# Attention, MoE and soft MoE on one core: the second pair's norm, the third pair's squares, two weight blocks and the first output block moved

## The chip, the cores and the metric

The kernel runs on one core of a Trainium2 chip. The time is device microseconds from the launch's start to its end on that core; a run is compared with other runs of the same kernel by the median. The engines are PE (TensorE, matrix products), DVE (VectorE), ACT (ScalarE), POOL (GpSimd) and SP (SyncE, which here only issues transfers). Transfers are issued from SP, ACT and POOL.

## What the reference computes

```python
# q, k, v: (4, 12, 448, 64); w_in (768, 2048), w_out (2048, 768); phi (768, 32); w1 (8, 768, 1024), w2 (8, 1024, 768)
q_n, k_n = rmsnorm(q, g_q), rmsnorm(k, g_k)
attn = softmax(q_n @ k_n.T / sqrt(64))          # with the row maximum subtracted
x = (attn @ v) as (1792, 768)
x = relu(x @ w_in) ** 2 @ w_out
logits = x @ phi
d = softmax over the 1792 tokens of logits       # dispatch
slot_input = d.T @ x                             # 32 slots, 4 for each of 8 experts
slot_out[e] = relu(slot_input[e] @ w1[e]) @ w2[e]
out = softmax over the 32 slots of logits @ slot_out
```

Everything is float32.

## The kernel before

**Attention** runs over 24 pairs of heads (4 batches, 6 pairs in each). A pair goes through these steps; the names are those of `blocks` in `attention()`:

- `load` brings q and k of a pair into two tiles `qk` (4 buffers, so a load waits until the norm has used the tiles of two pairs before).
- `norm` computes 1/rms. `inverse_rms` squares on ACT (line 250, tile `sq`, one buffer), reduces on DVE (252, `ss`), scales (258, `ms`), makes a first guess `y` by integer arithmetic on ACT (259), and takes three Newton steps of three DVE operations each (261 to 263). Then it multiplies q and k by y (302, `qs`). The first two pairs are done singly, later ones two at a time (`together`).
- `trans0`, `trans1` transpose on PE and make the operands of a head: `m1`/`m2` hold the rounded value of q and its remainder, `s1`/`s2` those of k with the gains. For the first pair `trans_first` does it: `m1` and its copy, `s1` and its remainder, then `gate` (a write that holds back the conversion of weights), then the "low" parts, `m2` on DVE (291) and `s2` on ACT (292). For later pairs the copies `m<-m` and `s<-s` are transfers on SP (331, 339).
- `max0`, `max1` (`rowmax`) compute the scores' row maxima: products on PE, a reduce on DVE (389, `nm`).
- `row0`, `row1` (`maxrow`) transpose the maxima (395), cast them (397, `mt`) and send them by a transfer into row 64 of `m2` (398), on ACT's queue for the first pair and on SP's for all others.
- `s00` to `s11` are the scores with the exponentials (411, tile `p`, 2 buffers), `v00` to `v11` the products with v, `recip` and `out` the division by the row sums.

`ORDER` and the first number in `blocks` set in which sequence the steps of neighbouring pairs are emitted. The framework's scheduler then fixes the order on each engine at compile time: it takes what was emitted first among what its own model of the times holds to be ready. So an instruction that was emitted late can stand early in an engine's queue, and on the chip the queue waits for it. Copies of a single element (248, 257, 364, 365) only exist to put one instruction behind another in this order.

**Weights.** `w_in` and `w_out` are fetched in 32 blocks of 768 KB by transfers on POOL's queue (`fetch64`), as raw words; `convert` turns a block into a high and a low part on ACT and DVE (553, 554, 560, 561), and SP writes these to scratch in DRAM. The list `CONVERT` says at which steps of attention a block is converted. The first four blocks (`PD`) are fetched with the first load, behind a one-element copy on POOL that waits for the first k. While attention goes on, the first layer (`moe_hidden`) is filled in between its steps, paced by `PACE`.

**The last part.** When attention's buffers are given back, three pools of buffers (`ring`, 18; `ring3`, 3; `ring2`, 5) take pieces of the weights in a fixed order, each piece in the buffer of one that is done (`done`, `fetch`). When no piece is left to fetch, `done` appends the pool to the list `free`. `finish` makes the output in 12 blocks `ob`, each in a buffer of the pool that it takes from the head of `free`; a block is copied out of PSUM in two halves by ACT and DVE (1158, 1156), and SP sends it (1159). By the order of the pieces the list begins with one entry of `ring`, then five of `ring2`, then five of `ring`, then `ring3`.

Of the kernel before, what the change touches and what calls it, by code (L numbers as in the profile page):

```python
# [8 lines left out]
F32 = mybir.dt.float32  # L9
# [11 lines left out]
def raw(ap):  # L21
    return ap.bitcast(F32)
# [19 lines left out]
VF, PD, LEAD, SLOPE = 9, 4, 1.5, 0.75  # L42
WF, EARLY, NTOP = 4, 1, 1
LAG, GATE, MTQ = 1, 1, 1
DUPE, HIP, SELG, VC, AHEAD = 0, 0, 1, 0, 1
FIRST = "load norm trans0 trans1 max0 max1 row0 row1 s00 s01 s10 s11".split()


ON_PL = [1, 0, 1, 1, 1, 1, 1, 1, 1, 1, 1, 0, 1, 0, 0, 1]
# [12 lines left out]
def tile_attention_moe_softmoe(  # L62
# [144 lines left out]
    def load_v(t):  # L207
        b, hp = divmod(t, NP)
        vh, vl = vst[t % 2]
        if t < VF:  # L210
            vf = att.tile([CP, 2, NC, D + 1], F32, tag="vr", name=f"vf_{t}", bufs=2)
            nc.vector.memset(vf[:, :, :, D:], 1.0)
            live[t]["vf"] = vf
            if VC:

                vr = att.tile([CP, 2, S], F32, tag="pl", name=f"vr_{t}", bufs=2)[:, :, : NC * D]
                nc.sync.dma_start(vr, v[b, 2 * hp : 2 * hp + 2].rearrange("h (p c) d -> p h (c d)", c=NC))
                nc.gpsimd.tensor_copy(vf[:, :, :, :D], vr.rearrange("p h (c d) -> p h c d", c=NC))
                return
            for j in range(2):  # L220
                nc.sync.dma_start(
                    vf[:, j, :, :D], v[b, 2 * hp + j].rearrange("(p c) d -> p c d", c=NC)
                )
            return
        vr = att.tile([CP, 2, NC, D + 1], F32, tag="vr", name=f"vr_{t}", bufs=2)
        vr = vr.rearrange("p h c d -> p (h c d)")[:, : 2 * NC * D].rearrange("p (h c d) -> p h c d", h=2, c=NC)
        nc.sync.dma_start(
            vr.rearrange("p h c d -> p h (c d)"),
            v[b, 2 * hp : 2 * hp + 2].rearrange("h (p c) d -> p h (c d)", c=NC),
        )  # L230
        for j in range(2):
# [9 lines left out]
    def inverse_rms(ts):  # L241
        n = 16 * len(ts)
        ss = att.tile([CP, 32], F32, tag="ss", name=f"ss_{ts[0]}", bufs=1)[:, :n]
        for x, t in enumerate(ts):
            for i in range(2):
                sq = att.tile([CP, 8, D], F32, tag="sq", name=f"sq_{t}_{i}", bufs=1)
                if AHEAD and t == 1 and i == 0:
                    nc.vector.tensor_copy(sq[0:1, 0, 0:1], live[0]["qs"][1][0:1, 0, 0, 0:1])
                qf = live[t]["qk"][i].rearrange("p h c d -> p (h c) d")
                nc.scalar.activation(sq, qf, AF.Square)  # L250
                at = 16 * x + 8 * i
                nc.vector.tensor_reduce(ss[:, at : at + 8], sq, AX.X, ALU.add)  # L252
        ms = att.tile([CP, 32], F32, tag="ms", name=f"ms_{ts[0]}", bufs=1)[:, :n]
        y = att.tile([CP, 32], F32, tag="y", name=f"y_{ts[0]}", bufs=2)[:, :n]
        u = att.tile([CP, 32], F32, tag="u", name=f"u_{ts[0]}", bufs=1)[:, :n]
        if AHEAD and ts[0] == 1:
            nc.vector.tensor_copy(ms[64:65, 0:1], raw(operands(0, 1)["s1"][64:65, 0:1]))
        nc.vector.tensor_scalar(ms, ss, 1.0 / D, EPS, ALU.mult, ALU.add)
        nc.scalar.activation(y.bitcast(I32), ms.bitcast(I32), AF.Copy, bias=float(0x5F3759DF), scale=-0.5)
        for _ in range(3):  # L260
            nc.vector.scalar_tensor_tensor(u, y, -0.5, y, ALU.mult, ALU.mult)
            nc.vector.tensor_tensor(u, u, ms, ALU.mult)
            nc.vector.scalar_tensor_tensor(y, u, 1.5, y, ALU.add, ALU.mult)
        for x, t in enumerate(ts):
            live[t]["y"] = y[:, 16 * x : 16 * x + 16]


    def trans_first():
        pss = []
        for i in range(2):  # L270
            ps = mps()
            x = live[0]["qs"][i]
            for c in range(NC):
                nc.tensor.transpose(
                    ps[:, c * CP : (c + 1) * CP], x[:, c].rearrange("p h d -> p (h d)"), ident[:CP, :CP]
                )
            pss.append(ps)
        for j in range(2):
            o = operands(0, j)
            h = slice(64 * j, 64 * j + 64)  # L280
            m, s, g = pss[0][h, :S], pss[1][h, :S], gkq[h, :]
            nc.scalar.copy(o["m1"][0:64, :], m)
            nc.vector.tensor_copy(o["m1"][64:128, :], m)
            nc.scalar.activation(o["s1"][0:64, :], s, AF.Copy, scale=g)
            nc.vector.scalar_tensor_tensor(o["s1"][64:128, :], s, g, raw(o["s1"][0:64, :]), ALU.mult, ALU.subtract)
        if GATE:
            gate(raw(o["s1"][64:65, 0:1]))
        for j in range(2):
            o = operands(0, j)
            h = slice(64 * j, 64 * j + 64)  # L290
            nc.vector.tensor_tensor(o["m2"][0:64, :], pss[0][h, :S], raw(o["m1"][0:64, :]), ALU.subtract)
            nc.scalar.activation(o["s2"][0:64, :], pss[1][h, :S], AF.Copy, scale=gkq[h, :])

    def norm(t):
        ts = together(t)
# [20 lines left out]
    def trans(t, i):  # L316
# [6 lines left out]
        for j in range(2):  # L323
            o = operands(t, j)
            src = ps[64 * j : 64 * j + 64, :S]
            if i == 0:
                nc.scalar.copy(o["m1"][0:64, :], src)
                if t < DUPE:
                    nc.scalar.copy(o["m1"][64:128, :], src)
                else:  # L330
                    small(t).dma_start(raw(o["m1"][64:128, :]), raw(o["m1"][0:64, :]))
                nc.vector.tensor_tensor(o["m2"][0:64, :], src, raw(o["m1"][0:64, :]), ALU.subtract)
            else:
                g = gkq[64 * j : 64 * j + 64, :]
                nc.scalar.activation(o["s1"][0:64, :], src, AF.Copy, scale=g)
                if t < DUPE:
                    nc.vector.tensor_scalar(o["s2"][0:64, :], src, g, None, ALU.mult)
                else:
                    small(t).dma_start(raw(o["s2"][0:64, :]), raw(o["s1"][0:64, :]))
# [3 lines left out]
                if GATE and t == 0 and j == 1:  # L343
                    gate(raw(o["s1"][0:1, 0:1]))


    def gate(src):
# [2 lines left out]
    def gains():  # L350
        for half in range(2):
            nc.scalar.dma_start(gkq[64 * half : 64 * half + 64, :], g_k.rearrange("(d o) -> d o", o=1))
            nc.scalar.dma_start(gq2[64 * half : 64 * half + 64, :], g_q.rearrange("(d o) -> d o", o=1))
        if SELG:
            nc.gpsimd.tensor_tensor(gkq, gkq, gq2, ALU.mult)
            nc.gpsimd.tensor_tensor(gkq, gkq, gsc, ALU.mult)
        else:
            nc.vector.scalar_tensor_tensor(gkq, gkq, scale, gq2, ALU.mult, ALU.mult)

    def selectors():  # L360
        nc.sync.dma_start(phi_sb, phi.rearrange("(kc p) s -> p kc s", p=128))
        if SELG:
            behind = raw(operands(0, 1)["s1"][64:68, 0:2])
            nc.vector.tensor_copy(i4[64:68, 0:2], behind)
            nc.vector.tensor_copy(seln, behind)
# [125 lines left out]
    def attention():  # L491
        for t in range(-3, NT + 1):
            for key in ORDER:
                dt, cost, run = blocks[key]
                if AHEAD and t + dt == 0 and key in ("trans0", "trans1"):
                    pass
                elif 0 <= t + dt < HIP and key in FIRST:
                    with tc.high_priority(offset=0):
                        run(t + dt)
                elif 0 <= t + dt < NT:  # L500
                    run(t + dt)
                if 0 <= t + dt < NT:
                    if AHEAD and t + dt == 0 and key == "norm":
                        trans_first()
                    if t == -3:
                        gains()
                        for u in units[:PD]:
                            fetched[u] = fetch64(*u, after=live[0]["qk"][1])
                    if t == 0 and key == "load":
                        selectors()  # L510
                    if key == "out" and (t + dt + 1) % NP == 0 and t + dt + 1 < NT:
# [16 lines left out]
    def fetch64(kind, fc, after=None):  # L528
# [3 lines left out]
            w64 = w64s[state["w64"]]  # L532
            state["w64"] ^= 1
        if after is not None:
            nc.gpsimd.tensor_copy(w64[0:1, 2:3], after[0:1, 0, 0, 0:1].bitcast(I32))
# [625 lines left out]
    for e in range(E):  # L1161
        for x in range(3 if e >= E - NL else 4):
            expert_out(e, x)
    finish(0, CA)
    for e in range(E - NL, E):
        expert_out(e, 3)
# [38 lines left out]
```

## Time and profile before

| | |
|---|---|
| median of 3 runs | 817.96 us (817.86 to 824.54) |
| the profiled execution | 818.53 us |
| its span, first to last instruction | 816.3 us |
| PE busy | 735.7 us (90%) |
| DVE busy | 502.0 us (61%) |
| ACT busy | 394.6 us (48%) |
| POOL busy | 116.0 us (14%) |
| moved by DMA | 184.76 MB |

The busy times are sums over the whole span, and the stages differ: a share of 90% does not say that PE sets the time in each of them. "Idle before" in a row is the time that the engine stood still just ahead of the instruction, and the arrow names what ended it.

### The profile page before, as it was taken

The page shows a single profiled execution, that of the slowest core. Times are in us where ns is not written, and L with a number is a line of the kernel's source. Part 1 is how long each engine was busy: PE and PEld are TensorE (multiplying, and loading weights), DVE is VectorE, ACT ScalarE, POOL GpSimd, SP SyncE. Part 2 cuts the span into 40 slices and gives each one's busy share as a digit, 9 for nine tenths or more (in the row PEclk, how much of TensorE's full clock was granted, in tenths as well). Part 3 has the DMA queues.
Part 4 walks back from the last instruction along what each step waited for, and adds up shares of the span by engine and source line. Part 5 has one row for each costly group of instructions (what it writes and reads, how often), then busy time and mean ns, then how long its engine had stood idle before and what let it go on. Part 6 is the DMA issues. An engine that isn't in the chain of part 4 may idle for free.

```text
span 816.3 us, 11544 instructions
## 1 busy us (share of the span) xinstructions
PE 735.7 (90%) x4030; PEld 517.0 (63%) x4030; DVE 502.0 (61%) x959; ACT 394.6 (48%) x666; POOL 116.0 (14%) x116
## 2 busy tenths in 40 slices
PE   2587878899999999999999999999999999988783
PEld 1354645567777877677877858787867887434121
DVE  7777868785589879878687688767236123220012
ACT  3657756665556766466665765555412112020012
POOL 3011110101110211312212323222200000000000
PEclk9998999999999999999999999999999999999897
DMA  8787977958776653354444424433336997999998
GB/s 242 251 311 240 305 206 265 276 159 276 255 242 201 193 166 106 96 161 141 139 137 157 124 74 121 142 101 101 117 125 265 415 414 295 412 416 414 395 331 266
DMA packets 76632, 184.76 MB, mean 226 GB/s; under 512 B 19200, under 2 KB 44064, under 8 KB 76576
## 3 DMA queue, kind: packets, MB, share of 16 engines
q1 hardware_dynamic: 70368, 158.64, 56.7%
q0 software_dynamic: 5632, 25.17, 9.6%
q8 instruction: 32, 0.52, 0.3%
q10 hardware_dynamic: 576, 0.23, 0.1%
q14 instruction: 24, 0.20, 0.1%
HBM read 148.73 MB, written 24.38 MB: 212 GB/s over the span
## 4 chain that ended last, share of the span: by engine, by line
PE 73%; DMA 7%; ACT 4%; DVE 4%; SPq 3%; issue 1%; DVEq 0%; ACTq 0%
PE ph L153 27%; PE pv L153 13%; PE pss L153 12%; PE pm L153 7%; PE pe L153 4%; PE pm L714 3%; DMA m<-m 3%; DMA w<-in_moe_w_dram 2%; PE pm L320 1%; SPq L980 1%; PE pt L153 1%; PE so_ps L153 1%; SPq L977 1%; DMA wi_s<-wh 1%; ACT p L411 1%
## 5 line engine op out<-in xcount | busy, mean ns | idle before, releaser
L153 PE MATMUL ph<-xh,whl 128*128 128x448 f32 x900 | 217.8, 374 | 2.0 <-ACT gt L746 2.0
L153 PEld LDWEIGHTS ph<-xh,whl 128*128 128x128 f32 x900 | 166.0, 188 | 23.4 <-ACT gt L746 4.8
L389 DVE TENSOR_REDUCE nm<-pss 112x2 f32<-112x896 f32 x96 | 102.6, 1086 | 21.6 <-PE pss L153 20.8
L153 PE MATMUL pss<-m,s 65*112 65x448 f32 (+1 forms) x384 | 108.4, 400 | 6.6 <-DMA m<-mt 4.4
L411 ACT ACTIVATE p<-pss 112x896 f32<-112x896 f32 x96 | 87.3, 917 | 53.0 <-PE pss L153 51.7
L153 PEld LDWEIGHTS pss<-m,s 65*112 65x112 f32 (+1 forms) x384 | 68.4, 184 | 27.5 <-issue 5.9
L746 ACT ACTIVATE gt<-ph 128x448 f32<-128x448 f32 x64 | 34.7, 543 | 90.1 <-PE ph L153 88.6
L153 PE MATMUL pss<-s,m 128*112 128x448 f32 x192 | 61.6, 418 | 18.5 <-DMA m<-m 6.0
L153 PE MATMUL pv<-ph,vst 112*65 112x448 f32 x240 | 71.9, 378 | 0.0
L153 PE MATMUL pv<-p,vf 112*65 112x448 f32 x144 | 67.3, 582 | 2.5 <-ACT p L411 2.5
L416 DVE TENSOR_TENSOR pl<-p,ph 112x896 fp32r<-112x896 f32 x42 | 47.7, 1135 | 20.2 <-ACT ph L415 18.7
L153 PEld LDWEIGHTS pss<-s,m 128*112 128x112 f32 x192 | 32.7, 186 | 38.8 <-issue 13.7
L415 ACT ACTIVATE ph<-pss 112x896 fp32r<-112x896 f32 x60 | 55.0, 916 | 3.8 <-PE pv L153 3.2
L754 POOL TENSOR_TENSOR gt<-gt 128x448 f32<-128x448 f32 x29 | 28.7, 991 | 195.8 <-ACT gt L746 187.8
L754 DVE TENSOR_TENSOR gt<-gt 128x448 f32<-128x448 f32 x30 | 19.5, 649 | 58.1 <-ACT gt L746 58.0
L153 PE MATMUL ph<-xh,wi 128*128 128x448 f32 x252 | 54.1, 369 | 0.0
L416 POOL TENSOR_TENSOR pl<-p,ph 112x896 fp32r<-112x896 f32 x18 | 38.2, 2125 | 111.4 <-ACT ph L415 95.8
L153 PEld LDWEIGHTS ph<-xh,wi 128*128 128x128 f32 x252 | 46.5, 188 | 3.5
L153 PE MATMUL pv<-pl,vst 112*65 112x448 f32 x120 | 44.6, 372 | 0.1
L437 ACT COPY t<-pv 65x448 f32<-65x448 f32 x48 | 25.1, 523 | 39.8 <-PE pv L153 39.6
L252 DVE TENSOR_REDUCE ss<-sq 112x8 f32<-112x512 f32 x48 | 32.4, 675 | 17.5 <-ACT sq L250 17.2
L250 ACT ACTIVATE sq<-qk 112x512 f32<-112x512 f32 x48 | 30.2, 630 | 26.6 <-DMA qk<-in_q_dram 14.7
(177 smaller groups left out, 1054.2 us busy)
## 6 DMA issues: line engine op xcount, KB each, us to landing
w<-in_moe_w_dram SPq DMA_DIRECT2D x60, 768.0 KB
whl<-wi_s SPq DMA_DIRECT2D x50, 768.0 KB
w<-in_moe_w_in_dram POOLq DMA_DIRECT2D x16, 768.0 KB, 6.5
w<-in_moe_w_out_dram POOLq DMA_DIRECT2D x16, 768.0 KB, 7.5
wi<-wi_s SPq DMA_DIRECT2D x14, 768.0 KB
wi_s<-wh SPq DMA_DIRECT2D x16, 384.0 KB
wi_s<-wf SPq DMA_DIRECT2D x16, 384.0 KB
wo_s<-wf SPq DMA_DIRECT2D x16, 384.0 KB
```

The source lines that it names most:

```text
L153: nc.tensor.matmul(o, lhsT, rhs, start=start, stop=stop)
L250: nc.scalar.activation(sq, qf, AF.Square)
L252: nc.vector.tensor_reduce(ss[:, at : at + 8], sq, AX.X, ALU.add)
L320: nc.tensor.transpose(ps[:, c * CP : (c + 1) * CP], x[:, c].rearrange("p h d -> p (h d)"), ident[:CP, :CP])
L389: nc.vector.tensor_reduce(nm[:, 2 * half : 2 * half + 2], ps[:CP, :, :S], AX.X, ALU.max, negate=True)
L411: nc.scalar.activation(p, ps[:CP, :, :S], AF.Exp)
L415: nc.scalar.activation(ph, ps[:CP, :, :S], AF.Exp)
L416: engine(ON_PL[t // NP * 4 + 2 * j + half]).tensor_tensor(pl, p, raw(ph), ALU.subtract)
L437: nc.scalar.copy(tt[: D + 1, j, :], ps[: D + 1, :S])
L714: nc.tensor.transpose(ps[:CP, fi * 128 : (fi + 1) * 128], gt[fi][:, c * CP : (c + 1) * CP], ident)
L746: nc.scalar.activation(gt, ps[:, :S], AF.Relu, scale=1.0 / UP)
L754: (nc.vector if k else nc.gpsimd).tensor_tensor(gt, gt, gt, ALU.mult)
```

## The change

It has four parts, and a clean-up of switches that changes no instruction.

1. `trans_first` becomes `first_pair`. Behind the first pair's operands it now also emits the second pair's norm, then for each head the row maxima, the low parts and the row. They are left out where the loop came to them before (`FIRST`). The second pair's squares are put behind the first pair's first guess `y` on ACT (by a copy of one element of it, `y0`), where they stood behind its finished `qs`; its second square takes a buffer of `p`, so it needn't wait for the first one's reduce; its reduces are put behind the first pair's `qs` on DVE. The copy that put its `ms` behind the last operand is gone.
2. The third pair's first square is put behind the second pair's finished `y`.
3. Of the first four weight blocks only two are fetched with the first load (`PD0`); the other two wait for the first head's operand `s1`.
4. The head of `free` is put at its end before the output is made.

```diff
+PD0, SQ2, MAXF = 2, 1, 1
+FIRST = ((0, "trans0"), (0, "trans1"), (0, "max0"), (0, "max1"), (0, "row0"), (0, "row1"), (1, "norm"))
...
             for i in range(2):
-                sq = att.tile([CP, 8, D], F32, tag="sq", name=f"sq_{t}_{i}", bufs=1)
-                if AHEAD and t == 1 and i == 0:
-                    nc.vector.tensor_copy(sq[0:1, 0, 0:1], live[0]["qs"][1][0:1, 0, 0, 0:1])
+                if (t, i) == (1, 1):
+                    sq = att.tile([CP, 2, S], F32, tag="p", name="sq_1_1", bufs=2).rearrange("p i s -> p (i s)")
+                    sq = sq[:, : 8 * D].rearrange("p (c d) -> p c d", d=D)
+                else:
+                    sq = att.tile([CP, 8, D], F32, tag="sq", name=f"sq_{t}_{i}", bufs=1)
+                if SQ2 and t == 2 and i == 0:
+                    nc.vector.tensor_copy(sq[0:1, 0, 0:1], live[1]["y"][0:1, 0:1])
                 qf = live[t]["qk"][i].rearrange("p h c d -> p (h c) d")
+                if (t, i) == (1, 0):
+                    nc.scalar.copy(sq[0:1, 0, 0:1], live[0]["y0"])
                 nc.scalar.activation(sq, qf, AF.Square)
+                if (t, i) == (1, 0):
+                    nc.vector.tensor_copy(ss[0:1, 0:16], live[0]["qs"][1][0:1, 0, 0, 0:16])
                 at = 16 * x + 8 * i
                 nc.vector.tensor_reduce(ss[:, at : at + 8], sq, AX.X, ALU.add)
...
-        if AHEAD and ts[0] == 1:
-            nc.vector.tensor_copy(ms[64:65, 0:1], raw(operands(0, 1)["s1"][64:65, 0:1]))
         nc.vector.tensor_scalar(ms, ss, 1.0 / D, EPS, ALU.mult, ALU.add)
         nc.scalar.activation(y.bitcast(I32), ms.bitcast(I32), AF.Copy, bias=float(0x5F3759DF), scale=-0.5)
+        if ts[0] == 0:
+            y0 = att.tile([1, 1], F32, tag="y0", name="y0", bufs=1)
+            nc.scalar.copy(y0, y[0:1, 0:1])
+            live[0]["y0"] = y0
...
-    def trans_first():
+    def first_pair():
...
         if GATE:
-            gate(raw(o["s1"][64:65, 0:1]))
-        for j in range(2):
+            gate(raw(operands(0, 1)["s1"][64:65, 0:1]))
+
+        def low(j):
             o = operands(0, j)
             h = slice(64 * j, 64 * j + 64)
+            nc.scalar.activation(o["s2"][0:64, :], pss[1][h, :S], AF.Copy, scale=gkq[h, :])
             nc.vector.tensor_tensor(o["m2"][0:64, :], pss[0][h, :S], raw(o["m1"][0:64, :]), ALU.subtract)
-            nc.scalar.activation(o["s2"][0:64, :], pss[1][h, :S], AF.Copy, scale=gkq[h, :])
+
+        norm(1)
+        if not MAXF:
+            low(0)
+            low(1)
+        for j in range(2):
+            rowmax(0, j)
+            if MAXF:
+                low(j)
+            maxrow(0, j)
...
-                elif 0 <= t + dt < NT:
-                    run(t + dt)
-                if 0 <= t + dt < NT:
-                    if AHEAD and t + dt == 0 and key == "norm":
-                        trans_first()
+                if 0 <= t + dt < NT:
+                    if (t + dt, key) not in FIRST:
+                        run(t + dt)
+                    if t + dt == 0 and key == "norm":
+                        first_pair()
+                        for u in units[PD0:PD]:
+                            fetched[u] = fetch64(*u, after=raw(operands(0, 0)["s1"][64:65, 0:1]))
                     if t == -3:
                         gains()
-                        for u in units[:PD]:
-                            fetched[u] = fetch64(*u, after=live[0]["qk"][1])
+                        for u in units[:PD0]:
+                            fetched[u] = fetch64(*u, after=live[0]["qk"][1][0:1, 0, 0, 0:1])
...
     for e in range(E):
         for x in range(3 if e >= E - NL else 4):
             expert_out(e, x)
+
+    free.append(free.pop(0))
     finish(0, CA)
```

## Rows read from the trace of the kernel before

**Rows 1.** The page's busy tenths in 40 equal slices of the span, PE and DMA.

```profile
PE   2587878899999999999999999999999999988783
...
DMA  8787977958776653354444424433336997999998
```

**Rows 2.** Windows by stage: length, busy time (instructions) by engine, PE clock, DMA share, GB/s.

```profile
26.00:28.00 2.00, 0.72 (x2) 0.40 (x2) 1.91 (x10) 0.23 (x1) 0.24 (x1) 1.00 0.00 1
...
60.00:160.00 100.00, 82.64 (x376) 52.60 (x375) 76.19 (x137) 66.78 (x108) 10.15 (x16) 0.91 0.84 258
160.00:600.00 440.00, 434.07 (x2313) 334.30 (x2312) 325.09 (x594) 259.56 (x425) 91.43 (x71) 1.00 0.49 153
```

**Rows 3.** Timeline, ACT, 11 to 36 us: start, length, instruction, idle before and releaser.

```profile
11.79 0.63 ACT L250 ACTIVATE sq<-qk 112x512 f32<-112x512 f32 x1 [3.48 <-DVE sq L248]
...
20.18 0.63 ACT L250 ACTIVATE sq<-qk 112x512 f32<-112x512 f32 x1 [4.94 <-DMA qk<-in_q_dram]
...
35.74 1.05 ACT L553 ACTIVATE top<-w 128x768 f16<-128x768 bf16 x1
```

**Rows 4.** Timeline, DVE, 12 to 31 us.

```profile
12.45 0.69 DVE L252 TENSOR_REDUCE ss<-sq 112x8 f32<-112x512 f32 x1 [0.75 <-ACT sq L250]
...
15.79 0.69 DVE L285 SCALAR_TENSOR_TENSOR s<-pm,gkq,s 64x448 fp32r<-64x448 f32 x1
...
19.35 1.08 DVE L389 TENSOR_REDUCE nm<-pss 112x2 f32<-112x896 f32 x1
...
23.28 0.18 DVE L261 SCALAR_TENSOR_TENSOR u<-y 112x16 f32<-112x16 f32 x1 [2.85 <-ACT y L259]
...
26.25 0.94 DVE L554 SCALAR_TENSOR_TENSOR wf<-w,top 128x768 int32<-128x768 int32 x1
...
27.31 0.16 DVE L364 COPY i<-s 4x2 f32<-4x2 f32 x1
...
29.06 1.27 DVE L302 TENSOR_TENSOR qs<-qk,y 112x512 f32<-112x512 f32 x2
```

**Rows 5.** Timeline, transfers issued from POOL, SP and ACT, and PE behind them.

```profile
8.45 2.65 POOL L539 DMA_DIRECT2D w<-in_moe_w_in_dram  x3
...
11.01 0.33 SPq L200 DMA_DIRECT2D qk<-in_q_dram  x1
...
25.83 1.90 ACTq L398 DMA_DIRECT2D m<-mt  x2
...
27.60 2.58 PE L153 MATMUL pss<-m,s 65*112 65x448 f32 x6 [1.28 <-DMA m<-mt]
...
29.80 0.31 SPq L200 DMA_DIRECT2D qk<-in_q_dram  x1
...
40.84 1.81 PE L153 MATMUL pss<-s,m 128*112 128x448 f32 x4 [4.12 <-DVE s L340]
...
52.28 1.46 SPq L398 DMA_DIRECT2D m<-mt  x2
...
56.57 1.49 PE L153 MATMUL pss<-m,s 65*112 65x448 f32 x6 [0.74 <-DMA m<-mt]
```

**Rows 6.** The chain that ended last, 54 to 153 us: start, length, what.

```profile
54.81 3.48 DMA m<-m
...
99.88 9.30 DMA m<-m
...
145.22 7.16 DMA m<-m
```

**Rows 7.** Timeline, DVE and SP, from 792 us, and a window.

```profile
792.13 0.69 DVE L1156 COPY ob<-pe 112x512 f32<-112x512 f32 x1 [1.29 <-PE pe L153]
...
793.40 1.96 DVE L1156 COPY ob<-pe 112x512 f32<-112x512 f32 x3 [0.57 <-PE pe L153]
...
794.75 15.75 SPq L1159 DMA_DIRECT2D out_dram<-ob  x12
...
794.00:796.00 2.00, 2.00 (x12) 0.97 (x12) 1.48 (x4) 1.12 (x3) 0.00 (x0) 1.00 0.26 76
```

More of the change, by code (lines that the diff above doesn't have):

```diff
@@ L44 @@
 LAG, GATE, MTQ = 1, 1, 1
-DUPE, HIP, SELG, VC, AHEAD = 0, 0, 1, 0, 1
-FIRST = "load norm trans0 trans1 max0 max1 row0 row1 s00 s01 s10 s11".split()
+PD0, SQ2, MAXF = 2, 1, 1
+FIRST = ((0, "trans0"), (0, "trans1"), (0, "max0"), (0, "max1"), (0, "row0"), (0, "row1"), (1, "norm"))
 ON_PL = [1, 0, 1, 1, 1, 1, 1, 1, 1, 1, 1, 0, 1, 0, 0, 1]
@@ L213, in load_v @@
             live[t]["vf"] = vf
[L214 to L219, printed above, removed]
             for j in range(2):
@@ L327, in trans @@
                 nc.scalar.copy(o["m1"][0:64, :], src)
[L328 to L331, printed above, removed]
+                nc.sync.dma_start(raw(o["m1"][64:128, :]), raw(o["m1"][0:64, :]))
                 nc.vector.tensor_tensor(o["m2"][0:64, :], src, raw(o["m1"][0:64, :]), ALU.subtract)
@@ L335, in trans @@
                 nc.scalar.activation(o["s1"][0:64, :], src, AF.Copy, scale=g)
[L336 to L339, printed above, removed]
+                nc.sync.dma_start(raw(o["s2"][0:64, :]), raw(o["s1"][0:64, :]))
                 nc.vector.scalar_tensor_tensor(
@@ L342, in trans @@
                 )
-                if GATE and t == 0 and j == 1:
-                    gate(raw(o["s1"][0:1, 0:1]))
     def gate(src):
@@ L353, in gains @@
             nc.scalar.dma_start(gq2[64 * half : 64 * half + 64, :], g_q.rearrange("(d o) -> d o", o=1))
[L354 to L358, printed above, removed]
+        nc.gpsimd.tensor_tensor(gkq, gkq, gq2, ALU.mult)
+        nc.gpsimd.tensor_tensor(gkq, gkq, gsc, ALU.mult)
     def selectors():
         nc.sync.dma_start(phi_sb, phi.rearrange("(kc p) s -> p kc s", p=128))
[L362 to L365, printed above, removed]
+        behind = raw(operands(0, 1)["s1"][64:68, 0:2])
+        nc.vector.tensor_copy(i4[64:68, 0:2], behind)
+        nc.vector.tensor_copy(seln, behind)
         nc.vector.tensor_tensor(i4, ident[:, 0:32], ident[:, 32:64], ALU.add)
@@ L494, in attention @@
                 dt, cost, run = blocks[key]
[L495 to L498, printed above, removed]
+                if 0 <= t + dt < NT:
+                    if (t + dt, key) not in FIRST:
                         run(t + dt)
-                elif 0 <= t + dt < NT:
-                    run(t + dt)
-                if 0 <= t + dt < NT:
-                    if AHEAD and t + dt == 0 and key == "norm":
-                        trans_first()
+                    if t + dt == 0 and key == "norm":
+                        first_pair()
+                        for u in units[PD0:PD]:
+                            fetched[u] = fetch64(*u, after=raw(operands(0, 0)["s1"][64:65, 0:1]))
                     if t == -3:
                         gains()
-                        for u in units[:PD]:
-                            fetched[u] = fetch64(*u, after=live[0]["qk"][1])
+                        for u in units[:PD0]:
+                            fetched[u] = fetch64(*u, after=live[0]["qk"][1][0:1, 0, 0, 0:1])
                     if t == 0 and key == "load":
@@ L534, in fetch64 @@
         if after is not None:
-            nc.gpsimd.tensor_copy(w64[0:1, 2:3], after[0:1, 0, 0, 0:1].bitcast(I32))
+            nc.gpsimd.tensor_copy(w64[0:1, 2:3], after.bitcast(I32))
         o = w64.bitcast(I16)[:, 1 : 1 + 4 * DM]
```

## The prediction

> **What bounds the kernel now.** I read the page first. Its busy tenths show TensorE (PE) full from slice 9 to 34 with gaps ahead of that, and DMA nearly full in the first ten slices and again from slice 31 [rows 1]. The windows by stage give the numbers [rows 2]: from 160 to 600 us PE is busy for 434.07 of 440 us, so nothing that the change touches can be won there; between 60 and 160 us it idles 17.4 of 100 us, with DMA at 0.84 of its time. In the last slices DMA streams the second layer's weights. That stream starts when attention's buffers are given back, so it comes earlier by whatever attention saves. Each engine's order is fixed at compile time; so I take it that a start shorter by x us moves everything behind it by x, unless the stretch from 60 to 160 us eats it.
>
> The timeline of the start, one engine after the other, gives the chain. VectorE (DVE) begins the last step of the first pair's operands at 15.79. It then does the m2 steps and two row maxima, and stands idle for 2.85 us until 23.28, waiting for ScalarE's (ACT's) seed y of the second pair's norm [rows 4]. ACT itself had stood idle 4.94 us, to 20.18: the square of the third pair's q headed its queue, and the load of that q, issued at 11.01, had to land first [rows 3, 5]. Behind that square stood s2 of the first pair, a conversion and the seed. So an early square of a pair that nobody needs yet holds the queue. Behind DVE's idle time come the second pair's scaled operands (29.06 for 1.27, so to 30.33), the load that reuses the buffers they free (29.80), and PE's first row-maximum products of the second pair, at 40.84 after idling 4.12 us [rows 4, 5].
>
> At the other end SP issues its first output transfer at 794.75, though the first DVE copy of an output block is done at 792.82 (792.13 + 0.69). The next three copies run from 793.40 for 1.96 us; 794.75 is the end of the second of these three, the third copy of all, and the block that heads SP's queue is the one copied third. DMA falls to 0.26 of its time in 794 to 796 [rows 7].
>
> **The change, part by part.** (1) *The second pair's squares right behind the first pair's seed.* ACT's two squares (0.63 each) leave their place among the operand copies, from 11.79 on, and run while DVE does its Newton steps; ACT idled 3.48 us there [rows 3], so they cost nothing. Without that cover they would cost 1.26. The second square now writes a buffer of the exponentials, which those need only behind the scores that start at 27.60 [rows 5]. The tiny copies that only fix an order are traded one for one: zero. DVE loses the 0.75 us idle ahead of the reduce at 12.45 [rows 4]. Bounds 0 and 0.75; I take 0.75, because the square was all that it waited for.
>
> (2) *The third pair's squares behind the second pair's finished norm.* Now nothing that waits for a load stands on ACT ahead of s2 and the seed, and DVE's 2.85 us go. What is late next is DVE's own work: row maxima of 1.08, Newton steps of 0.18, operands of 1.27 [rows 4]; it exists now and moves as a whole. The conversion step at 26.25 (0.94) and seven selector steps from 27.31 on (0.16 for the first, so about 1.1) stand ahead of the operands today [rows 4]. They are emitted later than the norm and may fall behind it: 0 to 2.1 us, of which I take half, 1.05, since DVE still owes them soon after. Behind the new wait stand, on DVE, one copy of a single element that follows the norm anyway, and on ACT the third pair's squares themselves; they are due with the fourth pair's, whose load (29.80) waits for the second pair's operands in any case [rows 5].
>
> (3) *Row maxima and rows of the first pair right behind, the low parts in between.* The same instructions in another order: 0. The rows' transfers stay on ACT's queue and pass no other load there, but leave earlier than at 25.83, into a fuller DMA system (the first rival).
>
> (4) *Two weight blocks later.* POOL issues weight blocks from 8.45 on, the first three in 2.65 us [rows 5]. Two of the four now wait on POOL for the first head's operand, which is finished before 15.79. Behind that wait stand only further weight blocks; those that need nothing may even be put ahead, which would undo the thinning. The third block is converted at 35.74 [rows 3], so it may take nearly 20 us to land. Nothing is lost; and after part (2) nothing on ACT waits for the load that is helped: 0.
>
> (5) *First output block from another pool.* If it is then copied first, SP issues at 792.82 instead of 794.75, 1.93 us earlier. DMA idles 0.74 of the 2 us from 794, 1.5 us, in that window alone, and the twelve issues then follow back to back for 15.75 us [rows 7], so the whole output moves. Bounds 0 (another block is held in its place) and 1.93; I take 1.9.
>
> Sum: 0.75 + 2.85 + 1.05 + 1.9 = 6.55. The profiled execution took 818.53 us, 816.3 of span and 2.2 around it; that gives 812.0. The median of the runs, 817.96, lies 0.57 lower, so the forecast is 811.5. Its own ends: parts (1) and the half of (2) at nothing, 813.2; 2.1 in full, 810.4.
>
> **The rivals.** *Start swallowed.* The first pair's scores need the rows that ACT sends at 25.83, and PE takes the first at 27.60: 1.77 us through a DMA system with 0.00 of its time busy in 26 to 28 [rows 2, 5]. In the changed kernel they leave some 5 us earlier, near 21 (an estimate: the 0.75, the 2.85, and somewhat more because the maxima no longer stand behind both m2 steps), while weight blocks are in flight. Today's q load, issued into such a crowd, took from 11.01 to 20.18, 9.17 us [rows 3, 5]; two rows of another pair, issued at 52.28, reached PE at 56.57, 4.29 us [rows 5]. With 4.29 the scores start near 25.3, still 2.3 earlier than now; with 9.17 near 30.2, 2.6 later, and the start gives nothing. With only the tail left this is 818.0 - 1.9 = 816, or 818.7 with 2.6 lost. For it: DMA is nearly full in the first slices [rows 1]. Against: the rows are tiny and go on another queue than the blocks. The Trainium skill (DMA: Bandwidth & Descriptors, Queues, rings and completion order) says that each DMA engine takes turns between its queues packet by packet, so a small transfer need not sit out another queue's backlog. By that rule this rival falls away; the q load's 9.17 us does not look like such turns and the later rows' 4.29 us does, so the trace leaves it open.
>
> *More than the sum.* The chain between 54 and 150 us runs through transfers of operand copies that wait in the crowd: 3.48, 9.30 and 7.16 us [rows 6]. If a new order frees the longest (9.30 down to 3.48), 5.8 us more go: 805.7.
>
> *The other way: new collisions.* The same stretch with the other sign. Every engine's order there is dealt anew, and a copy that takes 3.48 today can come to stand behind weight blocks. If the first and the third take 9.30 as well, that costs 5.8 + 2.1 = 7.9: 819.4, slower than before. It decides as soon as the collisions lengthen the chain by more than the 6.55 won; to pass 826, three must grow by 5.8 each. For it: DMA is at 0.84 of its time there [rows 2]. Against: the traffic is the same in amount.
>
> *The tail does not move.* The block is still not copied first: 813.4.
>
> **How the numbers follow.** Forecast 0.43 (811.5), start swallowed 0.18 (816 to 818.7), more than the sum 0.18 (805.7), new collisions 0.13 (819.4), tail unmoved 0.08 (813.4). One per cent, 8.2 us, is about what a measurement of this kernel can tell from no change: faster lies below 809.8, slower above 826.1. Faster over 1%: nearly all of the third case, and a quarter of the first, in which a little of the third comes too, 0.29. Slower over 1%: the worse third of the collisions, 0.05. Within 1%: 0.66. The range runs from 805.5 to 819: its lower end takes in one freed collision, its upper one a swallowed start and half of the new collisions; about 2 in 10 lie outside.
>
> **What would show it.** Right: ACT without the 4.94 us wait, DVE without the 2.85 us before the Newton steps, the second pair's operands done near 26 instead of 30.33, PE's products of 40.84 near 36; the first output transfer right behind the first DVE copy of a block, and no hole in DMA's share before it. The prediction goes wrong if the rows take long to reach PE, if the start is shorter but the gain is gone by 160 us, or if transfers of operand copies between 50 and 160 us are several us longer or shorter than today's.

## The result, and the profile after

| | median of the runs | lowest to highest | runs |
|---|---|---|---|
| before | 820.04 us | 817.86 to 824.54 | 4 |
| after | 830.65 us | 825.89 to 836.63 | 4 |

The ratio is 1.013 (95% interval 1.0086 to 1.0175): the change made the kernel slower by some 10.6 us, where 811.5 was forecast. The ratios here and below, with their intervals, are formed from the undisturbed runs and are not the quotients of the medians; the two can differ by 0.2% (0.9950 and 0.9935 for one kernel below). The profiled execution of after took 828.33 us, its span 826.1.

The page's busy tenths in 40 slices, PE and DMA:

```profile
PE   2578988789989999999999999999999999898774
...
DMA  8898878746676554254443433434245998999998
```

The windows by stage, with columns as in [rows 2]:

```profile
60.00:160.00 100.00, 83.15 (x378) 51.28 (x375) 75.39 (x137) 65.13 (x106) 9.90 (x15) 0.92 0.83 252
160.00:600.00 440.00, 428.88 (x2265) 328.89 (x2264) 322.34 (x587) 256.58 (x420) 89.68 (x69) 0.99 0.48 148
...
804.00:806.00 2.00, 2.00 (x9) 0.85 (x10) 1.29 (x2) 1.11 (x3) 0.00 (x0) 1.00 0.76 242
```

PE, which held nines from slice 9 on, now has an 8 in slices 9 and 12, and it is busy 5.19 us less in the stretch from 160 to 600 us than it was [rows 1, 2]. That stretch was the one in which I had said nothing could be won. I had not asked what could be lost there.

The timeline of the start, one engine after the other (ACT, DVE, PE, POOL):

```profile
16.30 0.22 ACT L259 ACTIVATE y<-ms 112x16 int32<-112x16 int32 x1 [0.23 <-DVE ms L258]
18.43 1.27 ACT L296 ACTIVATE s<-pm,gkq 64x448 fp32r<-64x448 f32 x2 [1.91 <-DVE s L289]
...
21.01 3.90 ACTq L401 DMA_DIRECT2D m<-mt  x2
27.73 0.92 ACT L414 ACTIVATE p<-pss 112x896 f32<-112x896 f32 x1 [6.72 <-PE pss L153]
...
18.43 0.18 DVE L265 SCALAR_TENSOR_TENSOR u<-y 112x16 f32<-112x16 f32 x1
...
24.28 0.94 DVE L554 SCALAR_TENSOR_TENSOR wf<-w,top 128x768 int32<-128x768 int32 x1
...
25.71 1.29 DVE L317 TENSOR_TENSOR qs<-qk,y 112x512 f32<-112x512 f32 x2
...
26.23 2.58 PE L153 MATMUL pss<-m,s 65*112 65x448 f32 x6 [2.30 <-DMA m<-mt]
...
34.66 0.92 PE L153 MATMUL pss<-s,m 128*112 128x448 f32 x2
...
8.58 2.65 POOL L539 DMA_DIRECT2D w<-in_moe_w_in_dram  x3
15.47 0.29 POOL L535 COPY w<-s 1x1 int32<-1x1 int32 x2 [4.24 <-DVE s L289]
15.71 0.56 POOL L543 DMA_DIRECT2D w<-in_moe_w_out_dram  x1
16.26 0.85 POOL L539 DMA_DIRECT2D w<-in_moe_w_in_dram  x1
17.10 0.56 POOL L543 DMA_DIRECT2D w<-in_moe_w_out_dram  x1
```

The start did what was forecast. ACT's 4.94 us wait for a load is gone, and so is DVE's wait of 2.85 us before the Newton steps (the first now runs at 18.43, with no wait ahead of it). The second pair's operands are done at 27.0 (25.71 + 1.29) instead of 30.33, and the first of the products that stood at 40.84 come at 34.66 [rows 3 to 5]. The row of the first head's maxima went into a crowd, as the first rival has it: from its issue at 21.01 to PE's products at 26.23 it took 5.2 us, where it had taken 1.77 [rows 5]. DMA was full (a share of 1.01 to 1.08) in each microsecond from 21 to 25, and at 0.55 in the next. PE still began these products 1.4 us earlier than before.

The tail (DVE, SP):

```profile
804.53 1.29 DVE L1156 COPY ob<-pe 112x512 f32<-112x512 f32 x2 [0.82 <-PE pe L153]
...
805.29 15.73 SPq L1159 DMA_DIRECT2D out_dram<-ob  x12
```

The first output transfer stands right behind the first of DVE's copies, whose pair began at 804.53; before, it stood behind the third [rows 7]. DMA's share around it is 0.76 and was 0.26.

So both ends were won, and the loss is in the middle. Starts of ACT's exponentials (four for each pair of heads), in us of each profiled span, date it:

| exponential | before | after | difference |
|---|---|---|---|
| 1st | 29.87 | 27.73 | -2.1 |
| 21st | 144.90 | 141.68 | -3.2 |
| 25th | 167.39 | 168.99 | +1.6 |
| 33rd | 217.45 | 223.64 | +6.2 |
| 41st | 269.18 | 281.12 | +11.9 |
| 45th | 295.75 | 306.35 | +10.6 |
| 93rd | 574.67 | 585.35 | +10.7 |

The start's lead holds to 145 us. Between 145 and 270 us some 15 us are lost (from 3.2 ahead to 11.9 behind), and behind that the distance stays as it is. In that stretch the windows read, before and after:

```profile
140.00:280.00 140.00, 133.78 (x680) 99.34 (x680) 105.35 (x194) 85.75 (x140) 17.73 (x20) 0.99 0.72 224
```

```profile
140.00:280.00 140.00, 126.59 (x610) 91.80 (x610) 96.47 (x176) 76.36 (x126) 13.32 (x16) 0.96 0.68 212
```

Every engine does less, PE 7.2 us less, and DMA does less too: nothing is fuller than it was, so they wait for one another. A part is TensorE's clock: in this window it stood at the lower of its two levels (0.5 of full, 1.2 GHz) for 10.2 us, 6.8 of them from 158.5 on, when PE had just idled 3.32 us; before, it did so for 3.4 us. If PE was busy all that while, the 6.8 us more at half speed cost at most some 3.4 of the 15 us (an estimate).

The chain of after (the work that ended last, followed back from the end, at each step to what released it) has these as its longest pieces there:

```profile
145.85 11.06 DMA wo_s<-wf
...
191.90 5.42 DMA qk<-in_k_dram
...
201.96 9.69 DMA w<-in_moe_w_in_dram
...
223.61 7.99 DMA wo_s<-wf
...
237.30 7.31 DMA wi_s<-wh
```

Four of the five belong to the weight conversion (its loads, and the writes that free its buffers). Before, the copy m<-m of 7.16 us stood at 145.22 [rows 6]; of the weight transfers only one of 4.02 us was on the chain between 140 and 280 us. The waits of after in 140 to 280 us (sum, times, longest) agree:

```profile
POOL w L539 <- DVE wf L554: 24.8, 3, 11.2
...
DVE wf L554 <- DMA wo_s<-wf: 10.1, 2, 6.1
```

The kernel before had these:

```profile
POOL w L539 <- DVE wf L554: 2.1, 1, 2.1
DVE wf L554 <- DMA wo_s<-wf: 1.8, 1, 1.8
```

POOL's row says less than it seems: before, POOL waited as well, with other instructions named at the end of the wait, and all its waits ahead of weight loads (L539, L543) come to 43.4 us before and 50.7 after. The waits of DVE's conversion step come to 2.0 and 11.7 us. One of them, on DVE and then on PE:

```profile
157.03 0.96 DVE L554 SCALAR_TENSOR_TENSOR wf<-w,top 128x768 int32<-128x768 int32 x1 [4.01 <-DMA wo_s<-wf]
157.90 2.08 DVE L392 TENSOR_REDUCE nm<-pss 112x2 f32<-112x896 f32 x2
...
159.04 0.71 PE L153 MATMUL pss<-m,s 128*112 128x448 f32 x1 [3.32 <-DVE nm L392]
```

The conversion step stands on DVE until the write of 11.06 us has given its buffer back; the row maxima stand behind it in DVE's queue, and PE idles for them. Between the 24th and the 25th exponential (156.92 and 167.39 us before, 152.58 and 168.99 after) 5.9 us are lost, more than in any other step.

### The profile page after: what moved, and what is told of

Same layout as the page of the kernel before. It is cut to its first block, busy times and chain, and to the rows that moved or that the text cites. A ratio compares the mean times of both kernels' runs of the same rounds, so it can differ in the third digit from the quotient of the medians.

```text
span 826.1 us, 11552 instructions
## 1 busy us (share of the span) xinstructions
PE 741.5 (90%) x4030; PEld 518.5 (63%) x4030; DVE 502.3 (61%) x959; ACT 394.2 (48%) x668; POOL 115.6 (14%) x116
## 4 chain that ended last, share of the span: by engine, by line
PE 63%; DMA 13%; ACT 5%; DVE 5%; SPq 3%; issue 3%; POOL 0%; DVEq 0%; ACTq 0%; POOLq 0%
PE ph L153 25%; PE pv L153 11%; PE pss L153 10%; PE pm L153 7%; DMA w<-in_moe_w_dram 5%; PE pm L714 3%; DMA wo_s<-wf 2%; PE pe L153 2%; SPq L980 1%; PE pm L335 1%; DMA w<-in_moe_w_in_dram 1%; DMA m<-m 1%; DMA qk<-in_q_dram 1%; ACT p L414 1%; SPq L977 1%
## 5 line engine op out<-in xcount | busy, mean ns | idle before, releaser
L153 PE MATMUL ph<-xh,whl 128*128 128x448 f32 x900 | 221.3, 377 | 4.2 <-ACT gt L746 4.1
L153 PE MATMUL so_ps<-w,hpad 128*32 128x256 f32 (+1 forms) x256 | 35.7, 530 | 9.6 <-DMA w<-in_moe_w_dram 9.3
L153 PEld LDWEIGHTS pv<-ph,vst 112*65 112x65 f32 x240 | 31.0, 136 | 14.8 <-issue 1.8
```

Source lines behind the costliest of these rows:

```text
L153: nc.tensor.matmul(o, lhsT, rhs, start=start, stop=stop)
```

## The experiments

*Theory.* Each engine's order is fixed when the kernel is built, by a scheduler that spreads the conversions among attention's steps. The change moves steps in the first 30 us; the scheduler deals most of what is behind them anew, up to some 290 us; the new order is the loss. *Rivals:* the operations of the change cost by themselves (the late blocks, the held-back squares); the earlier start runs into a weight stream that cannot come earlier, whatever the order; SP's queue, on which the weight writes stand behind the sums of the exponentials, is the place.

Beside the times I counted in the built programs how many pairs of instructions stand in another order than in the kernel before, over all five queues (the engines' orders, transfers included). The changed kernel has 2002. The times are medians, with that of before from the same chip beside it; the ratio is to before.

**The tail alone.**

```diff
+    free.append(free.pop(0))
     finish(0, CA)
```

> The kernel before with only the head of the free list moved to its end. The orders of all engines ahead of the last part are those of before. If the tail term of the forecast is right, the first output transfer starts within 0.1 us of the end of the first DVE copy of a block and the time falls by 1.9 us, a ratio of 0.998. If another block is held in its place, or the output moves no earlier because the transfers behind it fill the gap anyway: ratio 1.000.

820.73 us against 822.13, ratio 0.9983 (0.9961 to 1.0005); 38 pairs, nearly all in the tail. The gain is of the forecast's size and not told from nothing. Its queues ahead of the tail are those of before, and still its profiled execution fell some 5.5 us behind before's between 110 and 260 us: by that much one and the same order varies there from one execution to another.

**Four blocks at the old place, in the changed kernel.**

```diff
-PD0, SQ2, MAXF = 2, 1, 1
+PD0, SQ2, MAXF = 4, 1, 1
```

> The changed kernel with all four weight blocks fetched with the first load again. The orders on the engines stay nearly those of the changed kernel. Theory 'dealt order': what was lost between 145 and 270 us (12.9 us) comes from where the weight transfers and what waits for them stand in the queues, so it stays: ratio to before 1.010 to 1.016. Rival 'late blocks': the two blocks fetched later hold the conversions back; then the loss is gone and the start's gain shows: ratio 0.990 to 0.996.

832.35 against 822.13, 1.0114 (1.0076 to 1.0151), 2002 pairs. The late blocks are not the loss.

**The third pair's squares not held back, in the changed kernel.**

```diff
-PD0, SQ2, MAXF = 2, 1, 1
+PD0, SQ2, MAXF = 2, 0, 1
```

> The changed kernel without the copy that puts the third pair's first square behind the second pair's norm. By the forecast's own step ACT waits again for the third pair's q and the first pairs lose about 2.9 us of what they won, so the second pair's operands end near 30 instead of 27.0. Theory 'dealt order': the order behind is dealt anew as well, the stretch from 145 to 270 us changes by several us either way, and the total does not follow the 2.9: anywhere from 0.990 to 1.020. Rival 'a shorter start always shortens the whole': 1.013 + 0.0035 = 1.0165.

831.43 against 822.13, 1.0113 (1.0072 to 1.0153), 1777 pairs. The loss now comes in another place: the fifth exponential starts at 67.27, before at 57.48, and from 305 us on the distance is 14.6 to 14.8. Two thirds of it are there by the fifth exponential: the third pair's squares head ACT's queue again and stand for their loads, 5.13 us to 19.43 and 4.01 to 37.27.

**Only the third pair's squares held back, in the kernel before.**

```diff
                 sq = att.tile([CP, 8, D], F32, tag="sq", name=f"sq_{t}_{i}", bufs=1)
+                if t == 2 and i == 0:
+                    nc.vector.tensor_copy(sq[0:1, 0, 0:1], live[1]["y"][0:1, 0:1])
```

> The kernel before with only the copy that puts the third pair's first square behind the second pair's norm. The start wins the 2.85 us of DVE's idle time: second pair's operands at 27.5 instead of 30.33. Rival 'a shorter start shortens the whole': ratio 0.9965. Theory 'dealt order': the start wins 2.85 us and the total still moves by something else, as the stretch between 60 and 270 us is dealt anew: differences of 4 us and more between the gain at 30 us and the gain at 280 us.

826.65 against 822.13, 1.0044 (1.0011 to 1.0077), 1260 pairs. One copy of one element, with the first exponential 1 us earlier, and the kernel is slower.

**Only the two late blocks, in the kernel before.**

```diff
-                        for u in units[:PD]:
+                        for u in units[:2]:
...
+                        for u in units[2:PD]:
+                            fetched[u] = fetch64(*u, after=raw(operands(0, 0)["s1"][64:65, 0:1]))
```

> The kernel before with one part of the change: only two weight blocks are held back behind the first pair's operands (nothing of the norms' order, the tail as before). Theory 'dealt order' (each part re-deals the queues' orders between 60 and 270 us and so moves the time by anything up to some 10 us, mostly up since the order before was a chosen one): 820 to 832, a difference that is there at 60 to 270 us and constant behind 305 us. Rival 'the start is what counts' (less crowd at the start, first exponential earlier, all behind it as much earlier): 818 to 821. Rival 'late blocks' (fell with the run of four blocks): 830.

820.93 against 821.88, 0.9995 (0.9963 to 1.0026). The count of pairs is 0: this part deals nothing anew, and costs nothing. I had expected that each part would.

**Only part 1 of the change: the second pair's norm ahead, with the first pair's row maxima and rows behind its operands.**

```diff
-PD0, SQ2, MAXF = 2, 1, 1
+PD0, SQ2, MAXF = 4, 0, 1
...
-    free.append(free.pop(0))
```

> The changed kernel with the second pair's norm put early and nothing else of the change: all four weight blocks at the old place, the third pair's squares unbound, the output's first block as before. Theory 'dealt order': the first exponential 1.5 to 2.5 us earlier, yet 827 to 835 in time, with the loss arising between 60 and 270 us. Rival 'each part has its own price': 820 to 823, since the third pair's squares alone had cost 4.4 us, and the rest of the loss would lie in parts taken out here.

834.81 against 821.88, 1.016 (1.0119 to 1.0201), 1739 pairs. The time is as the theory has it, the rest is not: the first exponential starts at 32.16, not earlier, and the fifth at 67.95, 10.5 us late, so much of the loss is there before 68 us. Without the held-back squares a square heads ACT's queue again: it stands 6.60 us for a load of q, to 21.74, with operands of the first pair behind it, and another one 4.18 us, to 39.75.

**The sums on ScalarE's queue, in the kernel before and in the changed one.**

```diff
-            nc.sync.dma_start(
+            nc.scalar.dma_start(
                 live[t]["rsh"][16 * j : 16 * j + 16, :], tt[64:65, j, :].rearrange("o (r e) -> o r e", r=16)
```

> The kernel before; the sums of the exponentials go out on ScalarE's queue, which has just made them, not on SP's, where the issue stands for up to 7.8 us ahead of the weight writes. Theory 'the weight writes stand behind the sums in SP's order': 815 to 821 (before's order already has few such stands, 7.3 us in 140 to 280 us). Rival 'the writes are bound by the transfers themselves, not by SP's order': 820 to 824.

> The changed kernel; the sums of the exponentials go out on ScalarE's queue and not on SP's. Theory 'the weight writes stand behind the sums in SP's order' (23.5 us of such stands in 140 to 280 us): 5 to 12 us of the loss come back, 818 to 826, and the weight writes of wo and wi come 5 to 8 us earlier against the milestones. Rival 'transfers themselves' or 'any dealt order loses': 828 to 834, no nearer to before.

Before with it: 832.53 against 821.88, 1.0135 (1.0084 to 1.0186), 3677 pairs. After with it: 832.13, 1.0107 (1.0047 to 1.0167), 3187 pairs. The conversions of after did come earlier (the 26th at 185.77, not 187.71; the 27th at 194.40, not 200.71), and nothing was won: loads of q (10.22 us at 202.38) and an operand copy (7.97 at 229.05) stood on the chain in their place. Both times lie outside what the theory of SP's queue allowed, and before's outside its rival's range too. The runs do not rule SP's queue out as a place, for this edit also deals the orders anew; and SP's stands on the sums go with the order: 7.3 us from 140 to 280 us in before and 23.5 in after, 5.9 and 24.7 in the two kernels with exchanged orders below. What they show is that taking the sums off SP's queue does not bring the time back.

**Half of the weight loads left out, in both kernels.**

```diff
-                o.rearrange("p (kc f x) -> p kc f x", kc=KC, x=4), src[:, :, fc * 128 : (fc + 1) * 128, :]
+                o.rearrange("p (kc f x) -> p kc f x", kc=KC, x=4)[:, : KC // 2], src[:, : KC // 2, fc * 128 : (fc + 1) * 128, :]
...
+        nc.gpsimd.memset(o[:, 2 * DM :], 0)
```

> The kernel before with half of each weight block's load left out (the other half is zeros, written by GpSimd), so that the stretch from 60 to 270 us carries some 12 MB less by transfer; everything else is done. Theory 'the weight stream bounds the stretch from 60 to 270 us': 785 to 812 us, since the DMA share of 0.73 to 0.85 there falls and the waits on weight transfers go. Rival 'TensorE bounds the stretch': 815 to 825. The pair with the next run counts.

> The changed kernel with the same half of each weight block's load left out. Theory 'the weight stream takes back the start's gain and more': with half the stream the changed kernel is 2 to 6 us faster than the kernel before with half the stream (the start's 2 us and the tail's 2 us come through). Rival 'the dealt order itself costs, by collisions of attention's own transfers and waits between the engines': the changed kernel stays 5 to 14 us slower than its partner.

809.31 against 820.73, 0.9878 (0.9806 to 0.995), and 815.43, 0.9937 (0.9903 to 0.9971). Half the stream gives before 11.4 us, so the stream does bound some of the stretch; but the changed kernel stays 6.1 behind its partner, 5 by the ratios. With the whole stream it is 10.6. That a fuller DMA system makes the new order dearer is suggested by this and not shown, as the two intervals overlap.

**A control: the conversions from the seventh on two steps later, in both kernels.**

```diff
+CONVERT = [c + 2 * (c > 40) for c in CONVERT]
```

> A control: the kernel before with the conversions from the seventh on two steps of the list later (some 2.6 us); no work is added or taken out, and the start and the tail are as they were. Theory 'any re-dealing of the order in the stretch from 60 to 270 us costs, since the list was chosen for this order': 824 to 836. Rival 'only the change's own operations cost': 819 to 823.

> The changed kernel with the conversions from the seventh on two steps of the list later, which gives the weight transfers back the 2 to 3 us that the earlier start took from them. Theory 'attention came earlier and the weight transfers did not, so the order's conversions stand waiting': 818 to 825, most of the loss gone. Rival 'dealt order, no sense in it': anywhere from 822 to 838, as likely worse as better than the 830 of the change.

Before with it: 836.49 against 820.73, 1.0191 (1.0125 to 1.0256), 3187 pairs, with no work added and nothing of the change in; its chain holds other transfers than after's (one weight load of 7.82 us among them), so not every new order loses at the same steps. After with it: 830.98, 1.0115 (1.0051 to 1.0179), 3177 pairs; shifting the conversions by the lead that attention had won does not help.

**The first conversion at step 15, not 13.** This one entry of the list puts the changed kernel's queues back: 156 pairs instead of 2002, in the start and the tail alone; of VectorE's 959 instructions none stands elsewhere from the 83rd to the output's copies. In the kernel before, the same entry deals an order nearer to the changed kernel's (899 pairs from it) than to its own old one (1987).

```diff
-    13, 16, 16, 18, 27, 34, 46, 48, 54, 58, 58, 61, 63, 76, 86, 88,
+    15, 16, 16, 18, 27, 34, 46, 48, 54, 58, 58, 61, 63, 76, 86, 88,
```

> The changed kernel with the first weight conversion at step 15 of the list, not 13, and nothing else. In the built programs this puts the queues behind the first 80 rows of VectorE back into the order of the kernel before (156 pairs of instructions out of order against before, almost all in the start and the tail; the changed kernel has 2002). Theory 'the dealt order is the whole loss': the start's 2 to 3 us and the tail's 2 us come through, 814 to 819, faster than before. Rival 'the earlier start itself runs into the weight transfers, whatever the order': 824 to 832.

> The kernel before with the first weight conversion at step 15, not 13, and nothing of the change. In the built program this deals the queues' order anew: 1987 pairs out of order against before, 899 against the changed kernel. Theory 'the dealt order is the whole loss': 826 to 836, as slow as the changed kernel, though nothing of it is in. Rival 'the change's own operations cost': 818 to 823.

After with it: **817.07** against 822.42, 0.995 (0.9915 to 0.9985), faster than both kernels: 5.35 us by the medians, 4.1 by the ratio. Before with it: **834.86**, 1.0154 (1.0103 to 1.0205). The windows from 140 to 280 us, the changed kernel in before's order first, the kernel before in the other order second:

```profile
140.00:280.00 140.00, 134.28 (x689) 99.69 (x689) 106.75 (x196) 86.85 (x142) 17.70 (x20) 1.00 0.73 226
```

```profile
140.00:280.00 140.00, 126.48 (x612) 89.75 (x611) 97.62 (x177) 78.31 (x128) 12.46 (x15) 0.95 0.67 210
```

Each has the figures of the kernel whose order it shares, and not of the one whose operations it shares: 134.28 beside 133.78, 126.48 beside 126.59. So do the exponentials: from the 21st to the 41st after loses 15.2 us on before, the kernel before in the other order 14.5 (149.02 to 287.83), and the changed kernel in before's order loses nothing (144.88 to 267.40, 1.8 won). Another 4.1 us of the kernel before in the other order are lost ahead of the 21st. The chains say the same. The transfers longer than 5 us on that of the changed kernel in before's order, from 140 to 280 us:

```profile
145.21 6.39 DMA m<-m
...
226.54 6.65 DMA vr<-in_v_dram
...
277.97 5.36 DMA qk<-in_q_dram
```

and those on that of the kernel before in the other order:

```profile
153.22 11.88 DMA wo_s<-wf
...
198.24 5.38 DMA qk<-in_k_dram
...
208.30 9.31 DMA w<-in_moe_w_in_dram
...
242.38 8.74 DMA wi_s<-wh
```

These are four of the five pieces of after's chain (11.06, 5.42, 9.69, 7.31; the 7.99 is missing), in a kernel that holds nothing of the change. The waits of DVE's conversion step come to 9.6 us there, and to 1.4 in the changed kernel in before's order (11.7 in after, 2.0 in before). In both built programs the 25th and 26th conversion stand 12 instructions further ahead on VectorE than in before's order, and the 30th and 32nd 6 and 11.

**The same for the held-back squares alone.** The copy of the run with these squares stands in this kernel too; the first conversion goes to step 16 of the list, the third to 17.

```diff
-    13, 16, 16, 18,
+    16, 16, 17, 18,
```

> The kernel before with the third pair's first square behind the second pair's seed (this alone had 826.65) and the first weight conversion at step 17, which brings the order back near that of before (503 pairs out of order, against 1260 without it). Theory 'the dealt order is the whole loss': 818 to 823, the 4.4 us of that part gone. Rival 'holding the squares back has a price of its own': 825 to 829.

820.3 against 822.42, 0.9981 (0.995 to 1.0013), 503 pairs. The 4.5 us (826.65 against 822.13) that this part cost alone are gone with its order.

**In before's order: without the new tail, and with the four blocks at the old place.**

> The changed kernel with the first conversion at step 15 (817.07, 5.35 below before) and the output's first block from the old pool, so that the start stands alone in before's order. By the prediction's terms (start 4.65, tail 1.9): 817.8 to 819.2, some 2 us above the version with the tail and 3 to 5 below before. Rival 'the start's gain is gone by 160 us even in this order, and the gain came from the tail alone': 821 to 823.

> The changed kernel with the first conversion at step 15 and all four weight blocks at the old place (the orders of the engines stay the same). By the prediction's term (two blocks later: nothing): 816 to 818. Rival 'the thinned start is what brings the rows to TensorE earlier': 819 to 822, with the first exponential later than 27.46.

819.5 against 822.27, 0.9978 (0.9947 to 1.0009), and 817.9, 0.9958 (0.9925 to 0.9991). By the medians the start alone is worth some 2.8 us, and 1.8 by the ratio, whose interval includes zero; 819.5 lies just above the range expected. The tail gives 2.4 more (819.5 to 817.07, on two chips), the late blocks 0.8, with the first exponential 0.5 us later without them (27.96, not 27.46). These runs do not tell such differences from nothing.

Leaving the half loads aside, all fall in two groups. With at most 503 pairs out of order (six kernels) the medians lie between 817.07 and 820.93, each below before's beside it; with 1260 and more (nine, and the changed kernel itself) between 826.65 and 836.49. No kernel of one group lies in the other, whatever its edit. PE's busy time from 140 to 280 us parts them as well: 133.8 to 135.3 us in before and the six, 126.0 to 130.8 in the ten. Two of the ten, the ones without the held-back squares, lose much of it by the fifth exponential already.

## Why the prediction was wrong

**The step that failed** is the one sentence "I take it that a start shorter by x us moves everything behind it by x, unless the stretch from 60 to 160 us eats it", and with it the size and the place of the rival *New collisions*. That rival named the mechanism ("every engine's order there is dealt anew") and then priced it as two or three operand copies caught in a crowd before 160 us, 7.9 us in all, at a chance of 0.13. What the runs showed in its place: the order is dealt anew up to some 290 us, most of the long transfers that come onto the chain are the conversion's loads and writes, and the new order costs some 15 to 16 us (10.6 behind before as it stands, 4.1 to 5.35 ahead of it with before's order). The argument "the traffic is the same in amount" was true and proved nothing: DMA's share fell.

I had also taken the stretch from 160 us on for safe because PE was busy 434.07 of 440 us there [rows 2]. That says that nothing can be won, not that nothing can be lost; and the window from 140 to 280 us, in which PE idled 6.2 us and DMA stood at 0.72, I had not read by itself.

**(1) and (2), the start:** right in kind. Its signs came as forecast, the rows' slower way included (the rival's 4.29 us; 5.2 measured). So the row's way through a full DMA system lay nearer to that of the later rows than to the q load's 9.17. Forecast were 4.65 us, and the second pair's operands came 3.3 us earlier in after: of the conversion and selector steps that stood ahead of them the forecast took half as gone (1.05), but the conversion step (24.28) and two selector copies still stand there. In before's order the start gives 2.8 by the medians, 1.8 by the ratio (from 4.4 won to 0.7 lost). In the profile of the best version the first exponential is 2.4 us earlier (27.46), at 100 us nothing of that is there (101.46 against 100.54), and from 300 us on about 1.5 us are.

**(3) the reordered row maxima:** not tried alone. **(4) the late blocks:** nothing forecast, nothing found. As warned, blocks that need nothing were put ahead: POOL issues three from 8.58 on and three from 15.71 on, not two and two.

**(5) the tail:** 1.9 forecast, 1.4 and 2.4 measured, by kernels whose intervals reach 2 to 3 us either way.

So once the order is held the gain is 5.35 us by the medians and 4.1 by the ratio (1.2 to 7.0), and the sum of the terms, 6.55, lies within that interval. This does not confirm the terms one by one: neither the start's nor the tail's is told from nothing by itself. The changed kernel as it is has another order, and no term stood for that. The base was off as well: the profiled execution of before (818.53) was a quick one, and before's medians over 13 to 26 runs each were 820.73 to 822.42.

What stays open: which of the moved instructions costs how much, and why the scheduler deals the rest anew for two steps of one conversion. That the early conversions are what stands in the way is read from the chains, the waits and the equal places in two kernels; no run moved those alone, and it is not shown.

## What to carry to other kernels

Where a scheduler writes the order, an edit is two changes, its own and a new deal of everything behind it; before an edit is judged, compare the built queues with the old ones, and look for a setting that puts them back. The control that costs least is the old kernel in the new order: here it lost 12.4 us without any of the change. A busy engine bounds what can be won in a stretch, and says nothing of what a worse order can lose in it.

## What was not expected of the hardware

Executions of one built program differ by more than the effects under study: before ran from 815.19 to 828.78 us over the comparisons, and two kernels with the same order up to the tail lay 5.5 us apart from 290 us on, all of it from the stretch between 110 and 260 us in which transfers stand on the chain. A tiny transfer (one row of 448 numbers, issued at 21.01) took 5.2 us to its reader in the crowd of the start, and 1.77 in an empty system [rows 5].
